# Attention and a gated FFN in one kernel: the last pair's value copies, weight sums, batch order and event spacing changed

## The chip, the core and the metric

The kernel runs on one core of a Trainium2 chip. The metric is the device time of one execution in microseconds; three runs of the kernel before gave a median of 419.42 us (418.75 to 419.45).

## The reference

The inputs are q, k and v of 8 batches, 12 heads, 448 tokens and head dimension 64 (float32), and three weight matrices. What is computed:

```python
scores = q @ k.T / sqrt(64)                  # per batch and head
attn   = maximum(scores, 0) ** 2 / 448
x      = (attn @ v)                          # heads side by side: 3584 tokens x 768
gate   = maximum(x @ w_gate, 0)              # 768 -> 1536
val    = x @ w_val                           # 768 -> 1536
out    = (gate * val) @ w_out                # 1536 -> 768
```

There is no softmax: a ReLU and a square stand in its place, so the scores need no row sums, and all scale factors are put into later copies.

## The kernel before

All matmuls are in bf16 with float32 sums in PSUM, which is used as eight banks of 512 words (`banks`). Four matmuls that each use a quarter of TensorE's array (64 x 64) are issued together by `mm4`; four such matmuls over 448 columns are called a pass here.

**Scores and values.** A score event (`scores_event`, lines 670 and 232 to 251) is one pass into a pair of banks, a ReLU by ScalarE into a buffer `r_sb` (line 234), and a squaring by VectorE into an `attn` buffer (line 235). Seven score events make one quarter-batch unit (`qd`), of which a batch has three. A values event (`values_event`) is seven passes over `attn` and v into another pair of banks, and then copies out of PSUM into `x`. Both kinds of event take their banks from one rotation, banks 0-1 and 2-3 in turn (`sc_later`). So the second event after a values event needs the banks that the values were summed in. There are two `attn` buffers and four `r_sb` buffers.

Batches before 6 copy the values with `values` (line 265): ScalarE takes one bank, VectorE the other. Batches 6 and 7 use `values_by_parity` (line 272): even heads lie in the lower 64 partitions and odd heads in the upper 64. ScalarE copies the lower half of both banks (line 277) and VectorE the upper half of both (line 278); two more VectorE copies (279 and 280) repeat each result in the other half.

**Interleaving.** The stage of a batch runs through the gate and value units of the batch before (`gv_unit`, 12 units of 12 passes). Each unit sums into a pair of banks from the rotation 6-7, 4-5, and ends with a ReLU by ScalarE (line 321) and a product by VectorE (line 322) into `hT`. The events of the attention are put between the unit's passes at places that a function chooses ahead of time: `evenly` (line 704) spreads them by their number over the unit's passes, whether an event is one pass or seven. `spread` then issues everything in that order. Each engine's queue is in the order in which the program is written (`pin`). From batch 5 on, the scores and values of batches 5, 6 and 7 form one stream (`stream`, line 730), which the two last stages share.

**Loads.** `later_loads(b)` (line 722) is put at a place in a stage: two small copies by POOL that wait for the transposes of k and q (`hold`, line 683), then the loads of v for the next batch and of q and k for the one after, all issued by POOL.

**The output in block form.** For batches 2 and 3, 4 and 5, and 6 and 7, `out_pair` computes the output product with Winograd's scheme: seven block products in place of eight, at the price of sums of blocks. The blocks of `hT` are A11, A12 (the rows of the second half of d_ff) for the first batch's columns, and A21, A22 for the second's; `sums` (line 420) makes S1 = A21 + A22, A21 = A11 - A21, A11 = S1 - A11 and A12 = A12 - A11, each in two halves of rows by VectorE (line 422). Every product (`product`) is 12 matmuls for a tile of 128 tokens. ScalarE copies finished banks to an `attn` buffer (line 414), VectorE adds the other bank (line 418), and the result is stored from there by POOL, SP or, at the end, ScalarE's queue (`store_rows`, line 432). The `attn` buffers are then given to attention again. In the last pair the tokens are taken in two groups, tiles 0 and 1, then 2 and 3.

**The last pair in block form too.** `gv_pair` (line 510) does the gate and value products of batches 6 and 7 by the same scheme, in three groups of two units; each group is fourteen products of 24 matmuls. x11 to x22 are the blocks of the two batches' tokens (`token_sums`), a11 to a22 those of the weights, and s1, s2, s4 the weight sums (`block_sums`). The sums for the first group are made by VectorE during the output product before (line 792); those for the second and third group by POOL, at the start of the first and second group (`begun`, line 579). ScalarE keeps intermediate banks (line 540), and VectorE adds (line 544) and multiplies (545, 566) into `hT`.

Of the kernel before, what the change touches and what calls it, by code (L numbers as in the profile page):

```python
# [16 lines left out]
def kernel(  # L17
# [254 lines left out]
    def values_by_parity(b, qd, ps):  # L272

        value_passes(b, qd, ps, 0, NC)
        even, odd = (x_of[b][e][qd] for e in range(2))
        lo, hi = (p for _, p in HALVES)
        pin(nc.scalar.activation(even[lo], ps[lo, :, :S], AF.Copy, scale=float(lam)))
        pin(nc.vector.tensor_scalar(odd[hi], ps[hi, :, :S], float(lam), None, ALU.mult))  # L278
        pin(nc.vector.tensor_copy(even[hi], even[lo]))
        pin(nc.vector.tensor_copy(odd[lo], odd[hi]))  # L280
# [92 lines left out]

    def out_pair(b0, S1, extra=()):

# [6 lines left out]

        hT = hT_of[b0]
        A11, A12, A21, A22 = (hT[:, r * KH:r * KH + KH, c * S:c * S + S] for c in range(2) for r in range(2))
        tiles = [(t * 128, WHOLE) for t in range(S // 128)] + [(S - HALF, HALF)]
# [33 lines left out]

        def sums(o, a, b, op, s):  # L420
            for f in (slice(0, KH // 2), slice(KH // 2, KH)):
                pin(nc.vector.tensor_tensor(o[:, f, s], a[:, f, s], b[:, f, s], op))  # L422

        def store_rows(t, r, c0, c1, engines):
# [8 lines left out]

        pool, sync = ((e, e) for e in (nc.gpsimd, nc.sync))
        both, ends = (nc.gpsimd, nc.sync), (nc.sync, nc.scalar)
        for group in (((0, 1), (2, 3)) if last else ((0, 1, 2, 3),)):
            early = last and group[-1] == 3
            cols = slice(tiles[group[0]][0], sum(tiles[group[-1]]))
            sums(S1, A21, A22, ALU.add, cols)
            sums(A21, A11, A21, ALU.subtract, cols)  # L440
            for t in group:
                product(P, t, A11, B11, True)
                keep(t, 0, 0)
            sums(A11, S1, A11, ALU.subtract, cols)
            for t in group:
                product(Q, t, A12, B21, True)
                add(t, 0, 0)
                if early:
                    store_rows(t, 0, 0, 1, pool)
            sums(A12, A12, A11, ALU.subtract, cols)  # L450
            for t in group:
                product(P, t, A11, T2, False)
                keep(t, 0, 1)
                more(1)
# [3 lines left out]
            for t in group:  # L458
                product(P, t, A21, B12, False)
# [22 lines left out]
    def head_sums(o, a, b, op, engine):  # L482
        pin(engine.tensor_tensor(o, a, b, op))

    def token_sums(b0):

        x11, x21, x12, x22 = (x_of[b0 + j][e] for j in range(2) for e in range(2))
        t1, t2, t4 = (quads(flat(t, HP, S)) for t in (kn_b[0], qn_b[0], v_b[1]))
        ops = [[lambda q=q: head_sums(t1[q], x12[q], x11[q], ALU.subtract, nc.vector) for q in range(NQ)],
               [lambda q=q: head_sums(t2[q], x22[q], t1[q], ALU.subtract, nc.vector) for q in range(NQ)],  # L490
               [lambda q=q: head_sums(x12[q], x22[q], x12[q], ALU.subtract, nc.vector) for q in range(NQ)],
               [lambda q=q: head_sums(t4[q], x21[q], t2[q], ALU.subtract, nc.vector) for q in range(NQ)]]
        return (x11, x21, x22, t1, t2, x12, t4), ops
# [6 lines left out]

    def block_sums(m, s, engine):

        a11, a12, a21, a22 = blocks(m)
        s1, s2, s4 = s
        return [lambda: head_sums(s1, a21, a22, ALU.add, engine),
                lambda: head_sums(s2, s1, a11, ALU.subtract, engine),
                lambda: head_sums(a21, a11, a21, ALU.subtract, engine),
                lambda: head_sums(s4, a12, s2, ALU.subtract, engine)]

    def gv_pair(b0, xs, sets):  # L510

# [14 lines left out]
        for g in range(KF // 4):  # L526
            for op in (sets.begun(g) if g < 2 else ()):
                op()
            ms = (2 * g, 2 * g + 1)
# [6 lines left out]
            def out(n, i, c):  # L536
                return hT[:, 2 * ms[n] + i, c * S:c * S + S]

# [17 lines left out]
            for n in range(2):  # L556
                product(n, PQ[n][1], s[n][0], t1, True)
            for n in range(2):
                product(n, PQ[n][0], a[n][2], t3, False)
                keep(n, 2)  # L560
                add(n, 2, 1, 1)
            for n in range(2):
                product(n, PQ[n][0], a[n][3], t4, False)
                g_sb = gpool.tile([128, S], BF16, name="g_sb")
                pin(nc.scalar.activation(g_sb, banks[:, PQ[n][0], :S], AF.Relu))
                pin(nc.vector.tensor_tensor(out(n, 1, 0), banks[:, PQ[n][0] + 1, :S], g_sb, ALU.mult))  # L566
            for n in range(2):
                product(n, PQ[n][1], s[n][2], x22, False)
                add(n, 1, 0, 1)

    class Sets:
# [158 lines left out]
    def stream(b0, b1):  # L730

        e = []
        for b in range(b0, b1):
            for n in range(NT):
                if n % NC == 2 and (b, n) != (b0, 2):
                    vb, qd = (b, n // NC - 1) if n > NC else (b - 1, NQ - 1)
                    e.append((b, n, values_event(vb, qd)))
                e.append((b, n, scores_event(b, n)))
# [46 lines left out]
    def thirds(t):  # L785
        return [t[:, 2 * n:2 * n + 2, :].rearrange("p a s -> p (a s)")[:, 0:HP * 128].rearrange("p (g f) -> p g f", f=128)
                for n in range(3)]
# [3 lines left out]
                  .rearrange("p (g f) -> p g f", f=128) for _ in range(3)]])  # L791
    w0, w1 = (block_sums(m, sets.of(m), nc.vector) for m in range(2))
# [32 lines left out]
```

## Time and profile before

| | |
|---|---|
| median of three runs | 419.42 us (418.75 to 419.45) |
| profiled execution, whole | 420.81 us |
| its span, first to last instruction | 418.8 us |
| mean granted TensorE clock in the span | 0.993 |
| DMA traffic | 44.20 MB, mean 106 GB/s |
| stage of batches 5 to 7 | about 224.6 to 313.2 us |
| output block of batches 4 and 5 | about 313.2 to 337.2 us |
| gate and value pair of batches 6 and 7 | about 337.2 to 387.0 us |
| output block of batches 6 and 7, and tail | about 387.0 to 418.8 us |

The profile is one execution. PE is TensorE's matmuls and PEld its weight loads, DVE is VectorE, ACT ScalarE, POOL GpSimd, SP SyncE; a q behind a name (SPq, ACTq) is the engine's queue, where DMAs are issued. A row of the timeline has the start, the time from the first start to the last end, the engine, the line in the code, the operation and its tiles, the count, and in brackets the idle time of the engine ahead of it and who ended it. Neighbouring matmuls overlap, so the time of a row is longer than the distance to the next. A row of the chain (start, duration, what) can be a DMA on its way. A row of grouped instructions has the count, then the busy time and the mean in ns of one, then the idle time before.

### The profile page before, as it was taken

Reading aid. Unit: us, or ns where it says so; the run is one execution under the profiler, and the core shown is the slowest. Engines: PE = TensorE matmul, PEld = TensorE weight load, DVE = VectorE, ACT = ScalarE, POOL = GpSimd, SP = SyncE. Lnnn points to the kernel's source line nnn. Section 1 sums busy time; section 2 is a strip of 40 time slices with the busy share of each in tenths; the row PEclk is TensorE's granted clock in tenths of the full one; section 3 lists DMA queues with packets and bytes.
Section 4 is the critical chain, followed back from the end, with each engine's and each line's share of the span. In section 5 each row is a group of like instructions: output and inputs, shape, how many; then the busy total and the mean of one; then the engine's idle time right before and its main releaser. Section 6 shows DMA issues by size and latency. Waiting matters only on the chain.

```text
span 418.8 us, 17139 instructions
## 1 busy us (share of the span) xinstructions
PE 399.2 (95%) x7728; PEld 297.3 (71%) x7728; DVE 293.0 (70%) x493; ACT 243.3 (58%) x351; POOL 111.9 (27%) x155
## 2 busy tenths in 40 slices
PE   8899999999999999999999899999999999999894
PEld 4467777899887777777776577666667766677573
DVE  4985777347675998677924668887769966695651
ACT  4962886256765776886335678888773243334231
POOL 8823501250051410230007100020000189910030
PEclk9999999999999999999999999999999999999998
DMA  9999999989899793592709920750000170000053
GB/s 157 180 201 196 201 207 201 145 133 183 87 123 223 112 165 56 86 172 26 132 4 240 193 35 21 114 70 2 4 2 2 48 221 3 2 3 3 2 171 95
DMA packets 85929, 44.20 MB, mean 106 GB/s; under 512 B 54464, under 2 KB 83744, under 8 KB 85856
## 3 DMA queue, kind: packets, MB, share of 16 engines
q0 software_dynamic: 48704, 29.96, 48.5%
q1 hardware_dynamic: 36560, 12.66, 16.8%
q8 instruction: 60, 0.98, 1.0%
q10 hardware_dynamic: 592, 0.49, 0.5%
q14 instruction: 13, 0.11, 0.1%
HBM read 47.19 MB, written 11.01 MB: 139 GB/s over the span
## 4 chain that ended last, share of the span: by engine, by line
PE 63%; DMA 20%; DVE 7%; issue 4%; ACT 2%; POOL 2%; DVEq 0%; SPq 0%; POOLq 0%; ACTq 0%
PE ps L72 63%; DMA gv<-in_moe_w_val_dram 9%; DMA vn<-in_v_dram 5%; DMA out_dram<-attn 2%; DMA out_dram<-o_ring 2%; DVE kqT L544 2%; DVE hT L545 1%; DMA kn<-in_k_dram 1%; DMA kqT<-kr 1%; POOL vn L116 1%; POOL qn L116 1%; ACT r_sb L234 1%; DVE hT L566 1%; DVE x L278 1%; ACT kqT L540 0%
## 5 line engine op out<-in xcount | busy, mean ns | idle before, releaser
L72 PE MATMUL ps<-x,gv 64*64 64x448 bf16 x3648 | 209.1, 351 | 1.2 <-ACT o_ring L354 0.5
L72 PEld LDWEIGHTS <-gv 64*64 64x64 bf16 x4032 | 153.5, 107 | 48.4 <-issue 5.7
L234 ACT ACTIVATE r_sb<-ps 128x896 bf16<-128x896 f32 x168 | 148.8, 928 | 27.4 <-PE ps L72 24.3
L235 DVE TENSOR_TENSOR attn<-r_sb 128x896 bf16<-128x896 bf16 x168 | 102.6, 623 | 41.8 <-ACT r_sb L234 34.1
L72 PEld LDWEIGHTS <-hT 128*64 128x64 bf16 (+1 forms) x1536 | 71.9, 109 | 23.3 <-issue 2.7
L72 PE MATMUL ps<-kqT 64*64 64x448 bf16 x672 | 74.0, 353 | 8.2 <-ACT r_sb L234 2.4
L72 PE MATMUL ps<-wo,hT 64*64 64x384 bf16 (+2 forms) x1248 | 75.5, 315 | 0.8 <-issue 0.5
L322 DVE TENSOR_TENSOR hT<-ps,g_sb 128x448 bf16<-128x448 f32 x72 | 44.5, 619 | 13.9 <-ACT g_sb L321 13.5
L321 ACT ACTIVATE g_sb<-ps 128x448 bf16<-128x448 f32 x72 | 39.2, 546 | 23.3 <-PE ps L72 23.1
L414 ACT ACTIVATE attn<-ps 128x384 f32<-128x384 f32 (+1 forms) x48 | 21.7, 451 | 49.6 <-PE ps L72 49.6
L432 POOL DMA_DIRECT2D out_dram<-attn x24 | 13.1, 548 | 134.5 <-ACT attn L414 128.7
L72 PEld LDWEIGHTS <-kqT 64*64 64x64 bf16 x672 | 32.4, 107 | 21.3 <-issue 12.9
L72 PEld LDWEIGHTS <-vn 64*64 64x64 bf16 (+1 forms) x840 | 33.5, 107 | 10.0 <-issue 1.1
L72 PE MATMUL ps<-attn,vn 64*64 64x448 bf16 x672 | 38.3, 349 | 0.0
L418 DVE TENSOR_TENSOR attn<-ps,attn 128x384 f32<-128x384 f32 (+1 forms) x36 | 16.9, 502 | 23.1 <-ACT attn L414 14.1
L540 ACT ACTIVATE kqT<-ps 128x896 f32<-128x896 f32 x18 | 16.5, 918 | 26.7 <-PE ps L72 26.7
L683 POOL COPY flag<-kqT 128x1 bf16<-128x1 bf16 x12 | 2.8, 242 | 102.9 <-DMA kqT<-kr 70.2
L544 DVE TENSOR_TENSOR kqT<-ps,kqT 128x896 f32<-128x896 f32 x18 | 19.5, 1082 | 14.8 <-ACT kqT L540 11.4
L116 POOL DMA_DIRECT2D vn<-in_v_dram x36 | 23.6, 672 | 18.8 <-DMA wo<-in_moe_w_out_dram 9.9
L72 PE MATMUL ps<-o_ring,hT 128*64 128x384 bf16 (+1 forms) x288 | 22.2, 306 | 1.5 <-DVE hT L422 1.4
L268 ACT ACTIVATE x<-ps 128x448 bf16<-128x448 f32 x15 | 8.2, 544 | 17.8 <-PE ps L72 17.8
L263 DVE COPY x<-x 64x896 bf16<-64x896 bf16 x36 | 14.6, 407 | 2.0
(99 smaller groups left out, 299.4 us busy)
## 6 DMA issues: line engine op xcount, KB each, us to landing
out_dram<-attn SPq DMA_DIRECT2D x16, 192.0 KB, 4.6
out_dram<-attn POOLq DMA_DIRECT2D x16, 192.0 KB, 4.5
kn<-in_k_dram POOLq DMA_DIRECT2D x7, 384.0 KB, 8.0
qn<-in_q_dram POOLq DMA_DIRECT2D x7, 384.0 KB, 10.6
vn<-in_v_dram POOLq DMA_DIRECT2D x14, 192.0 KB, 7.8
out_dram<-o_ring POOLq DMA_DIRECT2D x14, 192.0 KB, 5.5
wo<-in_moe_w_out_dram POOLq DMA_DIRECT2D x2, 1152.0 KB, 16.9
kn<-in_k_dram POOLq DMA_DIRECT2D x7, 288.0 KB, 9.3
```

The lines of the kernel that those rows point to most:

```text
L72: pin(nc.tensor.matmul(o, lhsT=l, rhs=r, start=start, stop=stop, skip_group_check=True))
L116: pin(nc.gpsimd.dma_start(out=o, in_=i))
L234: pin(nc.scalar.activation(r, src, AF.Relu))
L235: pin(nc.vector.tensor_tensor(dst, r, r, ALU.mult))
L263: pin(nc.vector.tensor_copy(x1[p], x0[other]))
L321: pin(nc.scalar.activation(g_sb, o[0], AF.Relu, scale=float(out_scale)))
L322: pin(nc.vector.tensor_tensor(hT[:, mf, col:col + S], o[1], g_sb, ALU.mult))
L414: pin(nc.scalar.activation(out_of(t, r, c), bank(P, t), AF.Copy))
L418: pin(nc.vector.tensor_tensor(o, bank(Q, t), o, ALU.add))
L432: pin(engines[c].dma_start(out=rows[:, c0:c1, :], in_=src))
L540: pin(nc.scalar.activation(held(n, j), both(PQ[n][0]), AF.Copy))
L544: pin(nc.vector.tensor_tensor(k, both(PQ[n][1]), k, ALU.add))
```

## The change

- `values_by_parity`: for each half of the partitions ScalarE copies the first bank and VectorE the second, four copies of 64 x 448 in place of two of 64 x 896.
- The places of the events in the last two stages come from a new function, `paced`. It counts passes, one for a score, seven for a values event, one for each pass of a unit, and gives each score the same number of passes; a values event lies half a period behind the score before it, and the next score half a period behind that.
- `later_loads(5)` is put at the fifth unit of its stage in place of the third.
- `token_sums` takes the two batches of the last pair in the other order, and `gv_pair` writes the results to `hT` with the column blocks exchanged, so that the first batch's place in the scheme is taken by batch 7.
- The weight sums of the second and third group are VectorE's, later in the group: behind the products of s1 with t1. No sum is left to POOL.
- In the third group VectorE makes S3 = A11 - A21 and, in two parts, S1 for the first two token tiles. `out_pair` of the last pair then leaves these out and keeps S2 and S3 in tiles of their own (the places of t2 and t1), where A11 and A21 were overwritten.
- The last stores are given to other queues: the second batch's first column half of the last two tiles to ScalarE's queue alone (SP and ScalarE before), the first batch's second half of tile 2 to SP alone (SP and ScalarE before).

```diff
-        pin(nc.scalar.activation(even[lo], ps[lo, :, :S], AF.Copy, scale=float(lam)))
-        pin(nc.vector.tensor_scalar(odd[hi], ps[hi, :, :S], float(lam), None, ALU.mult))
+        for x, p in ((even, lo), (odd, hi)):
+            pin(nc.scalar.activation(x[p, 0, :], ps[p, 0, :S], AF.Copy, scale=float(lam)))
+            pin(nc.vector.tensor_scalar(x[p, 1, :], ps[p, 1, :S], float(lam), None, ALU.mult))
...
+    def half_sums(o, a, b, op, s, halves=(0, 1)):
+        for f in (slice(n * KH // 2, (n + 1) * KH // 2) for n in halves):
+            pin(nc.vector.tensor_tensor(o[:, f, s], a[:, f, s], b[:, f, s], op))
...
-        A11, A12, A21, A22 = (hT[:, r * KH:r * KH + KH, c * S:c * S + S] for c in range(2) for r in range(2))
+        A11, A12, A21, A22 = quarters(b0)
+        S2, S3 = apart or (A11, A21)
...
-            sums(S1, A21, A22, ALU.add, cols)
-            sums(A21, A11, A21, ALU.subtract, cols)
+            if not last:
+                half_sums(S1, A21, A22, ALU.add, cols)
+                half_sums(S3, A11, A21, ALU.subtract, cols)
+            elif early:
+                half_sums(S1, A21, A22, ALU.add, cols)
             for t in group:
                 product(P, t, A11, B11, True)
                 keep(t, 0, 0)
-            sums(A11, S1, A11, ALU.subtract, cols)
+            half_sums(S2, S1, A11, ALU.subtract, cols)
...
-                        store_rows(t, 1, 0, 1, ends)
+                        store_rows(t, 1, 0, 1, act)
...
-                        store_rows(t, 0, 1, 2, ends)
+                        store_rows(t, 0, 1, 2, sync if tiles[t][1] == WHOLE else ends)
...
-        x11, x21, x12, x22 = (x_of[b0 + j][e] for j in range(2) for e in range(2))
+        x11, x21, x12, x22 = (x_of[b0 + 1 - j][e] for j in range(2) for e in range(2))
...
         for g in range(KF // 4):
-            for op in (sets.begun(g) if g < 2 else ()):
-                op()
...
-                return hT[:, 2 * ms[n] + i, c * S:c * S + S]
+                return hT[:, 2 * ms[n] + i, (1 - c) * S:(2 - c) * S]
...
             for n in range(2):
                 product(n, PQ[n][1], s[n][0], t1, True)
+            if ms[1] < KF // 2 - 1:
+                for op in sets.begun(g):
+                    op()
+            else:
+                A11, A12, A21, A22 = quarters(b0)
+                begun = slice(0, 2 * WHOLE)
+                half_sums(S1, A21, A22, ALU.add, begun, (0,))
+                half_sums(S3, A11, A21, ALU.subtract, slice(0, S))
...
+            if ms[1] == KF // 2 - 1:
+                half_sums(S1, A21, A22, ALU.add, begun, (1,))
...
-            return [op for m in (2 * g + 2, 2 * g + 3) for op in block_sums(m, self.of(m), nc.gpsimd)]
+            return [op for m in (2 * g + 2, 2 * g + 3) for op in block_sums(m, self.of(m))]
...
+    def paced(units, u1, events):
+
+        places, todo, t = [], list(events), 0
+        at = [(u, n) for u in range(u1) for n in range(len(units[u]))]
+        scores = sum(passes == 1 for *_, passes in events)
+        period = (len(at) + sum(passes for *_, passes in events)) / scores
+        due = period / 2
+        for u, n in at:
+            while todo and t >= due:
+                *_, e, passes = todo.pop(0)
+                places.append((u, min(n, len(units[u]) - 4), e))
+                t += passes
+                due += period / 2 if todo and (passes > 1) != (todo[0][3] > 1) else period
+            t += 1
+        return places + [(u1 - 1, len(units[u1 - 1]) - 4, e) for *_, e, _ in todo]
...
-            events = evenly(units, 0, last + b % 2, [e for _, _, e in todo])
+            events = paced(units, last + b % 2, todo)
...
-        events.append(({2: 10, 5: 2}.get(b, 3), 1, lambda b=b: later_loads(b)))
+        events.append(({2: 10, 5: 4}.get(b, 3), 1, lambda b=b: later_loads(b)))
...
-    gv_pair(B - 2, xs, sets)
-    out_pair(B - 2, S1)
+    S2, S3 = (flat(t, KH, S) for t in (qn_b[0], kn_b[0]))
+    gv_pair(B - 2, xs, sets, S1, S3)
+    out_pair(B - 2, S1, apart=(S2, S3))
```

More of the change, by code (lines that the diff above doesn't have):

```diff
@@ L372, in weight_sums, with quarters, out_pair @@
         pin(nc.vector.tensor_tensor(o, a, b, op))
-    def out_pair(b0, S1, extra=()):
+    def half_sums(o, a, b, op, s, halves=(0, 1)):
+        for f in (slice(n * KH // 2, (n + 1) * KH // 2) for n in halves):
+            pin(nc.vector.tensor_tensor(o[:, f, s], a[:, f, s], b[:, f, s], op))
+    def quarters(b0):
+        hT = hT_of[b0]
+        return [hT[:, r * KH:r * KH + KH, c * S:c * S + S] for c in range(2) for r in range(2)]
+    def out_pair(b0, S1, extra=(), apart=None):
         last, extra = b0 == B - 2, list(extra)
@@ L432, in store_rows @@
                 pin(engines[c].dma_start(out=rows[:, c0:c1, :], in_=src))
[L434 removed]
+        pool, sync, act = ((e, e) for e in (nc.gpsimd, nc.sync, nc.scalar))
         both, ends = (nc.gpsimd, nc.sync), (nc.sync, nc.scalar)
@@ L449, in out_pair @@
                     store_rows(t, 0, 0, 1, pool)
-            sums(A12, A12, A11, ALU.subtract, cols)
+            half_sums(A12, A12, S2, ALU.subtract, cols)
             for t in group:
-                product(P, t, A11, T2, False)
+                product(P, t, S2, T2, False)
                 keep(t, 0, 1)
@@ L458, in out_pair @@
             for t in group:
-                product(P, t, A21, B12, False)
+                product(P, t, S3, B12, False)
                 keep(t, 1, 1)
@@ L477, in out_pair, with head_sums @@
                     if early:
-                        store_rows(t, 0, 1, 2, ends)
+                        store_rows(t, 0, 1, 2, sync if tiles[t][1] == WHOLE else ends)
                     else:
                         store_rows(t, 0, 0, 2, both)
-    def head_sums(o, a, b, op, engine):
-        pin(engine.tensor_tensor(o, a, b, op))
+    def head_sums(o, a, b, op):
+        pin(nc.vector.tensor_tensor(o, a, b, op))
     def token_sums(b0):
-        x11, x21, x12, x22 = (x_of[b0 + j][e] for j in range(2) for e in range(2))
+        x11, x21, x12, x22 = (x_of[b0 + 1 - j][e] for j in range(2) for e in range(2))
         t1, t2, t4 = (quads(flat(t, HP, S)) for t in (kn_b[0], qn_b[0], v_b[1]))
[L489 to L492, printed above, removed]
+        ops = [[lambda q=q: head_sums(t1[q], x12[q], x11[q], ALU.subtract) for q in range(NQ)],
+               [lambda q=q: head_sums(t2[q], x22[q], t1[q], ALU.subtract) for q in range(NQ)],
+               [lambda q=q: head_sums(x12[q], x22[q], x12[q], ALU.subtract) for q in range(NQ)],
+               [lambda q=q: head_sums(t4[q], x21[q], t2[q], ALU.subtract) for q in range(NQ)]]
         return (x11, x21, x22, t1, t2, x12, t4), ops
```

22 lines of the change are left out of this document (9 added, 13 removed).

## The prediction

> **What bounds the kernel now.** I read the page's shares and clock line first, then the windows view (where TensorE stands or runs slowly), then the timeline around each such place.
>
> ```profile
> span 418.8 us, 17139 instructions
> PE 399.2 (95%) x7728; PEld 297.3 (71%) x7728; DVE 293.0 (70%) x493; ACT 243.3 (58%) x351; POOL 111.9 (27%) x155
> 238.00:240.00 2.00, 1.26 (x16) 0.84 (x19) 1.85 (x5) 0.77 (x1) 0.00 (x0) 0.74 1.52 194
> 240.00:242.00 2.00, 2.00 (x28) 1.36 (x24) 1.43 (x3) 0.84 (x3) 0.00 (x0) 0.50 1.47 188
> 242.00:244.00 2.00, 2.00 (x44) 1.50 (x40) 0.63 (x1) 1.61 (x3) 0.00 (x0) 0.91 0.54 69
> 390.00:396.00 6.00, 4.58 (x58) 2.92 (x56) 4.79 (x11) 0.98 (x2) 0.00 (x0) 1.00 0.00 0
> ```
>
> TensorE is busy 95% of the span, so only its stalls and slow stretches can be won. In a windows row the columns are PE, PEld, DVE, ACT, POOL, granted clock, DMA share and GB/s. From 238 to 244 us the clock falls to 0.74, 0.50 and 0.91: 0.26 x 2 + 0.50 x 2 + 0.09 x 2 = 1.70 us of work lost. From 390 to 396 us TensorE also stands still, for 1.42 us, and the clock stays at 1.00. What stands ahead of the slow stretch:
>
> ```profile
> 224.59 0.57 PE L72 MATMUL ps<-x,gv 64*64 64x448 bf16 x8
> 227.43 8.72 DMA out_dram<-attn
> 229.62 1.33 PE L72 MATMUL ps<-x,gv 64*64 64x448 bf16 x24
> 230.75 0.39 PE L72 MATMUL ps<-kqT 64*64 64x448 bf16 x4
> 236.46 1.16 DVE L235 TENSOR_TENSOR attn<-r_sb 128x896 bf16<-128x896 bf16 x2 [3.56 <-DMA out_dram<-attn]
> 238.07 0.61 DVE L269 CAST x<-ps 128x448 bf16<-128x448 f32 x1
> 238.74 0.41 PE L72 MATMUL ps<-kqT 64*64 64x448 bf16 x2 [2.09 <-DVE x L269]
> ```
>
> The last store of the first block-form output (issued 227.43, 8.72 us on its way) holds an attention buffer. VectorE wants that buffer for the eighth score of batch 5, waits 3.56 us for it, and with it waits everything queued behind: two squarings, one gate product, the copy of the first values (L269). TensorE needs that copy's PSUM bank and starts again at 238.74. I call four matmuls a pass: 24 matmuls from 229.62 to 230.75, so 0.189 us a pass.
>
> **Part 1, events spaced by passes, stage of batches 5 to 7 (224.6 to 313.2 us).** In the built program's TensorE order, the score that stalls (the eleventh) comes after 61 passes now and after 67 in the changed kernel; the eighth score after 37 passes now, 48 then. Nothing ahead of the release changes: POOL's and SP's lists up to there, and what each entry waits for, are the same in both builds. So "one part's loads later" moves nothing (POOL is held by its own queue, not by the place in the source), the store still lands at 236.15, and L269 still ends near 238.69: eighth and ninth squaring, a gate product and L269 are queued on VectorE there in the new order too. TensorE arrives at 224.6 + 67 x 0.189 = 237.26 instead of 224.6 + 61 x 0.189 = 236.1. It has then done 6 passes more when it restarts at 238.74: **-1.13 us**. Its wait is 1.48 us. Of today's 2.6 us (236.1 to 238.74) 2.09 show as idle, since matmuls already issued run out first; of the 1.48 some 1.0 to 1.2 will, less than the 1.42 after which the clock stayed at 1.00: the slow stretch goes, **-1.70 us**.
>
> **Part 2, the values' copies and what follows them.**
>
> ```profile
> 264.17 1.52 PE L72 MATMUL ps<-attn,vn 64*64 64x448 bf16 x28
> 265.50 0.95 PE L72 MATMUL ps<-x,gv 64*64 64x448 bf16 x16
> 265.74 0.91 ACT L277 ACTIVATE kn<-ps 64x896 bf16<-64x896 f32 x1 [0.88 <-PE ps L72]
> 266.69 1.09 DVE L278 TENSOR_SCALAR kn<-ps 64x896 bf16<-64x896 f32 x1 [1.01 <-ACT kn L277]
> 267.83 0.38 PE L72 MATMUL ps<-kqT 64*64 64x448 bf16 x4 [0.81 <-DVE kn L278]
> 247.74 0.55 ACT L268 ACTIVATE x<-ps 128x448 bf16<-128x448 f32 x1 [0.79 <-PE ps L72]
> 247.78 0.63 DVE L269 CAST x<-ps 128x448 bf16<-128x448 f32 x1 [0.17 <-PE ps L72]
> 313.17 7.03 PE L72 MATMUL ps<-wo,hT 128*64 128x384 bf16 x96
> L234 ACT ACTIVATE r_sb<-ps 128x896 bf16<-128x896 f32 x168 | 148.8, 928 | 27.4 <-PE ps L72 24.3 <-ACT g_sb L321 1.2 <-ACT r_sb L234 0.8
> ```
>
> Today both engines read both banks, and VectorE begins (266.69) only when ScalarE has ended: the bank is free 2.33 us after the last value pass (265.50 to 267.83). Bank by bank they run side by side, as L268 and L269 do at 247.74. ScalarE needs two of 0.55, VectorE two of about 0.62 with some 0.07 of overlap, from 0.24 after the passes: free at 0.24 + 1.17 + 0.03 = 1.44 us. That is 0.9 us less. But the new spacing puts a score directly behind the value passes and the next, which needs their bank, one or two passes later; today ten to thirteen passes lie between. So the wait is not 2.33 - 1.32 = 1.01 any more, but 1.44 - 0.38 = 1.06 with one pass between (three times), 1.44 - 0.57 = 0.87 with two (once), 1.44 - 0.19 = 1.25 with none (batch 6, first): 5.30 together. Batch 5's second and third values keep the old copies (free at 0.24 + 0.63 + 0.03 = 0.90) and waited for nothing; now 0.90 - 0.38 = 0.52 and 0.90 - 0.57 = 0.33. For VectorE being late (regrouping copies and gate products in its queue) I add 0.60, an estimate of one L322 or so. New: 6.75 us of waits. Now: from 238.74 to the output block at 313.17 are 74.43 us for 414 - 61 = 353 passes x 0.189 = 66.7, so 7.7 lost, less the clock's 1.70: 6.0. Difference **+0.75 us**: faster copies, nearly all spent on closer neighbours. ScalarE and VectorE keep up between values: a score every 6.2 to 6.4 passes is 1.2 us, a ReLU 0.93.
>
> Stage: -1.13 - 1.70 + 0.75 = -2.08. Bounds: -3.0 (VectorE never late, shorter copies) and -0.4 (slow stretch stays).
>
> **Part 3, weight sums from POOL to VectorE (337 to 387 us).**
>
> ```profile
> 337.23 0.57 PE L72 MATMUL ps<-kn,gv 64*64 64x448 bf16 x8
> 353.80 0.95 PE L72 MATMUL ps<-kn,gv 64*64 64x448 bf16 x8
> 370.91 0.57 PE L72 MATMUL ps<-kn,gv 64*64 64x448 bf16 x8
> 387.01 1.17 PE L72 MATMUL ps<-wo,hT 128*64 128x384 bf16 x12
> 348.71 1.09 DVE L544 TENSOR_TENSOR kqT<-ps,kqT 128x896 f32<-128x896 f32 x1 [4.00 <-ACT kqT L540]
> 349.83 1.77 DVE L545 SCALAR_TENSOR_TENSOR hT<-kqT 128x448 bf16<-128x448 f32 x1
> 383.45 0.63 DVE L545 SCALAR_TENSOR_TENSOR hT<-kqT 128x448 bf16<-128x448 f32 x1
> 358.36 0.57 PE L72 MATMUL ps<-kn,gv 64*64 64x448 bf16 x8 [0.58 <-DVE kqT L544]
> 326.31 0.55 DVE L483 TENSOR_TENSOR x<-gv 128x768 bf16<-128x768 bf16 x1
> 328.43 1.15 DVE L483 TENSOR_TENSOR kr<-qr,kr 128x896 bf16<-128x896 bf16 x2
> ```
>
> The first three rows and 387.01 bound three equal groups: 16.57, 17.11 and 16.10 us. POOL works in the first two only, and there VectorE's L545 takes up to 1.77 us against 0.63 without POOL. VectorE falls behind and TensorE waits (358.36). Without POOL the first two should take 16.10 each: -0.47 - 1.01 = **-1.5 us**. VectorE gets eight sums a group: four took 328.43 - 326.31 = 2.12, so 4.24 us. They stand in its queue where it was idle for 4.00 us, after an L545 that gets 0.3 shorter: they fit, with some 0.6 us to spare before TensorE meets the next L544. If they didn't fit, up to 2.8 us (1.4 a group) would come back.
>
> **Part 4, start of the last output block, and tail.**
>
> ```profile
> 382.32 1.09 DVE L544 TENSOR_TENSOR kqT<-ps,kqT 128x896 f32<-128x896 f32 x1 [4.28 <-ACT kqT L540]
> L422 DVE TENSOR_TENSOR kn<-hT 128x1344 bf16<-128x1344 bf16 x2 | 1.6, 849 | 0.0
> 388.38 1.08 DVE L544 TENSOR_TENSOR kqT<-ps,kqT 128x896 f32<-128x896 f32 x1
> 390.03 1.02 DVE L422 TENSOR_TENSOR vn<-hT 128x768 bf16<-128x768 bf16 x2
> 392.51 1.65 PE L72 MATMUL ps<-o_ring,hT 128*64 128x384 bf16 x18 [1.42 <-DVE hT L422]
> 410.46 5.68 SPq L432 DMA_DIRECT2D out_dram<-attn  x8
> 411.62 2.96 ACTq L432 DMA_DIRECT2D out_dram<-attn  x4
> out_dram<-attn SPq DMA_DIRECT2D x16, 192.0 KB, 4.6
> ```
>
> Today six half sums follow the last hT row (390.1), and TensorE waits 1.42 us for the fifth. In the new order four of them lie earlier. S3 and half of S1 stand in VectorE's idle time before the third group's adds (4.28 us; 2 x 0.85 + 0.55 = 2.25 of sums). S3 overwrites t1 and so waits until TensorE has passed the group's eighth product, at 370.91 + 8 x 16.10/14 = 380.1 and a run-out of 0.2; it ends at 382.0, before 382.32, and behind it in the queue is the add that TensorE's last products need: 0.3 us to spare, and what S3 is late beyond that would come on top. The other half of S1 stands before the last adds, which end 0.5 later, at 390.6. Then two sums, until 391.6. But A12 now holds the rows made last: the first Q product (from 388.96, 12 matmuls in 1.17 less the run-out, 0.081 each) stops at its fifth row until 390.65, ends 391.0, its neighbour at 392.0, and the block that began at 392.51 begins there: **-0.5 us** (bounds -1.0 and +0.3). In the tail SP issues eight stores in 5.68 us, 0.71 each, and is last; one goes to ScalarE's queue. Alone that is -0.7, and nothing if the two queues take turns; I take **-0.4 us**. The Trainium skill, Perfetto Trace Analysis, section "DMA Instruction — HWDGE (DVE, Sync)", says that the descriptor generator is locked for one issuer at a time; by that the tail would give 0 and the sum 0.4 us less. No row here decides it.
>
> **Sum.** -2.08 - 1.5 - 0.5 - 0.4 = -4.5 us. The profiled execution is 418.8 us of span in 420.81 us; the median of the runs is 419.42, and the same difference is taken off it: **414.9 us**. A measurement of this kernel can tell about 0.2%, 0.84 us.
>
> **Rivals.**
> *A: the slow stretch stays.* The stores land at another moment than here, or 1.1 us of standing already halves the clock. For: nothing between 1.42 (held) and 2.09 us (halved) was seen, and the landing is a DMA's. Against: 1.42 held. 414.9 + 1.7 = 416.6 us, chance 0.13.
> *B: the loads do come later* and the store lands in the 4.6 us median of its kind (the row above): about 1 us more is won, 413.9 us. Against: the same POOL list. Chance 0.04.
> *C: VectorE becomes the bound in the pair*: 1.5 not won and 2.8 given back: 414.9 + 4.3 = 419.2, no change. For: VectorE would be busy almost all of two groups. Against: the idle slots of 4.0 us. Chance 0.04.
> *D: slower; the two halves of the copies still run one after the other* (a bank or a semaphore orders them as now). Then the bank is free at 2.33, and the five waits are 2.14 + 1.76 + 3 x 1.95 = 9.75 instead of 5.30: 419.35. TensorE stands for 1.75 us at three of them and 1.94 at one, beyond the 1.42 that was harmless; each halving costs 1.7, and with one the kernel is slower, with four 426.2. It decides from a copy of about 2 us on. Against: 247.74 shows the pair side by side. Chance 0.06. The Trainium skill, TensorE: Matmul & The Clock Gate, section "What's actually happening", has the clock fall only after about 3.4 us of idle window; by that D would stay at 419.35 and A would not exist. The 2.09 us of standing ahead of 0.50 contradict it, so D and A keep their prices.
>
> **How the numbers follow.** Forecast 0.73, A 0.13, B 0.04, C 0.04, D 0.06. The range 412.9 to 417.2 takes in the forecast with its bounds, A and B, and leaves C, D out. Faster by over 0.2%: forecast, A, B and a part of C, 0.91; within: 0.03; slower: 0.06.
>
> **What would show it.** Part 1: idle near 237 us of 1.0 to 1.3, clock 1.00 from 238 to 244. Part 2: ACT and DVE copies of 64x448 at the same time, and seven TensorE waits of 0.3 to 1.1 us (less the run-out) behind value passes. Part 3: no L545 over 0.65 us, groups of about 16.1 us, no TensorE wait for L544. Part 4: a wait of about 0.9 us inside the first Q product, none for S2; the last SP store issued some 0.5 us sooner against the last matmul. Wrong would be: a granted clock under 1 behind a value copy (D), L544 late in the pair (C), the store landing before 235 (B).

## The result, and the profile after

The changed kernel takes 414.63 us in the median (414.24 to 415.19), the kernel before beside it 419.43 us: ratio 0.989, 95% interval 0.9873 to 0.9908. The forecast was 414.9. The profiled execution took 414.38 us.

The page of the changed kernel, first its span and the shares of the engines, then the windows view around 238 us (columns as in the prediction):

```profile
span 412.6 us, 17150 instructions
PE 397.6 (96%) x7728; PEld 293.4 (71%) x7728; DVE 298.8 (72%) x513; ACT 245.3 (59%) x357; POOL 82.5 (20%) x139
236.00:238.00 2.00, 1.41 (x26) 0.69 (x22) 1.90 (x5) 1.35 (x2) 0.00 (x0) 1.00 1.55 192
238.00:240.00 2.00, 2.00 (x52) 1.50 (x44) 1.66 (x4) 1.46 (x2) 0.00 (x0) 1.00 1.48 196
240.00:242.00 2.00, 2.00 (x48) 1.51 (x44) 1.51 (x3) 1.76 (x4) 0.00 (x0) 1.00 1.23 153
```

TensorE still misses 0.59 us ahead of 238, but the clock stays at 1.00 where it was 0.74 and 0.50. Rows of the timeline and, for the store, of the chain, in order of time; the comparison by stage rests on their starts:

```profile
223.83 0.95 PE L72 MATMUL ps<-x,gv 64*64 64x448 bf16 x16
226.50 8.56 DMA out_dram<-attn
236.95 0.38 PE L72 MATMUL ps<-kqT 64*64 64x448 bf16 x2 [0.25 <-ACT x L268]
237.66 0.38 PE L72 MATMUL ps<-kqT 64*64 64x448 bf16 x2 [0.34 <-DVE x L269]
282.16 1.10 ACT L278 ACTIVATE x<-ps 64x448 bf16<-64x448 f32 x2 [0.61 <-PE ps L72]
282.34 1.27 DVE L279 TENSOR_SCALAR x<-ps 64x448 bf16<-64x448 f32 x2
283.31 0.73 PE L72 MATMUL ps<-kqT 64*64 64x448 bf16 x4 [0.64 <-ACT x L278]
310.16 2.14 PE L72 MATMUL ps<-wo,hT 128*64 128x384 bf16 x24
334.22 2.46 PE L72 MATMUL ps<-kr,gv 64*64 64x448 bf16 x48
350.25 2.47 PE L72 MATMUL ps<-kr,gv 64*64 64x448 bf16 x48
366.21 2.47 PE L72 MATMUL ps<-kr,gv 64*64 64x448 bf16 x48
382.31 2.79 PE L72 MATMUL ps<-wo,hT 128*64 128x384 bf16 x32
386.07 1.49 PE L72 MATMUL ps<-wo,hT 128*64 128x384 bf16 x16 [0.97 <-DVE hT L551]
387.39 2.12 PE L72 MATMUL ps<-o_ring,qn 128*64 128x384 bf16 x24
406.22 1.67 PE L72 MATMUL ps<-wo,hT 128*64 128x384 bf16 x24
405.32 4.60 SPq L437 DMA_DIRECT2D out_dram<-attn  x7
406.47 3.15 ACTq L437 DMA_DIRECT2D out_dram<-attn  x5
L551 DVE SCALAR_TENSOR_TENSOR hT<-kqT 128x448 bf16<-128x448 f32 x18 | 11.3, 625 | 0.6
345.70 1.09 DVE L550 TENSOR_TENSOR kqT<-ps,kqT 128x896 f32<-128x896 f32 x1 [0.35 <-ACT kqT L546]
```

| | before, us | after, us | difference | forecast |
|---|---|---|---|---|
| stage of batches 5 to 7 | 88.58 | 86.33 | -2.25 | -2.08 |
| output block of batches 4 and 5 | 24.06 | 24.06 | 0 | 0 |
| gate and value pair | 49.78 | 48.09 | -1.69 | -1.5 |
| start of the last output block to the first S2 product | 5.50 | 5.08 | -0.42 | -0.5 |
| start of the last product to the end of the span | 7.44 | 6.38 | -1.06 | -0.4 |

Together -5.42. The spans differ by 6.2; of the remaining 0.8, 0.76 is that the stage starts at 223.83 in place of 224.59. The change touches nothing ahead of it, and in the profiled executions below this start lies between 223.11 and 224.69 us, without regard to what was changed.

### The profile page after: what moved, and what is told of

It reads as the page before. It is cut to its first block, busy times and chain, and to the rows that moved or that the text cites. A ratio compares the mean times of both kernels' runs of the same rounds, so it can differ in the third digit from the quotient of the medians.

```text
span 412.6 us, 17150 instructions
## 1 busy us (share of the span) xinstructions
PE 397.6 (96%) x7728; PEld 293.4 (71%) x7728; DVE 298.8 (72%) x513; ACT 245.3 (59%) x357; POOL 82.5 (20%) x139
## 4 chain that ended last, share of the span: by engine, by line
PE 63%; DMA 18%; issue 11%; DVE 3%; POOL 2%; ACT 1%; DVEq 0%; POOLq 0%; ACTq 0%
PE ps L72 63%; DMA gv<-in_moe_w_gate_dram 7%; DMA wo<-in_moe_w_out_dram 4%; DMA vn<-in_v_dram 3%; DMA out_dram<-attn 3%; DMA kn<-in_k_dram 1%; DVE kqT L550 1%; POOL vn L116 1%; DVE hT L551 0%; POOL qn L116 0%; POOL out_dram L437 0%; POOL gv L116 0%; DVE hT L580 0%; ACT x L278 0%; ACT qr L278 0%
## 5 line engine op out<-in xcount | busy, mean ns | idle before, releaser
L72 PE MATMUL ps<-x,gv 64*64 64x448 bf16 x3552 | 201.6, 349 | 0.8 <-ACT r_sb L234 0.3
L234 ACT ACTIVATE r_sb<-ps 128x896 bf16<-128x896 f32 x168 | 150.2, 925 | 25.6 <-PE ps L72 22.4
L72 PE MATMUL ps<-kqT 64*64 64x448 bf16 x672 | 79.0, 351 | 6.2 <-ACT r_sb L234 2.2
L72 PEld LDWEIGHTS <-hT 128*64 128x64 bf16 (+1 forms) x1440 | 65.4, 109 | 21.4 <-issue 2.7
L72 PE MATMUL ps<-wo,hT 64*64 64x384 bf16 (+2 forms) x1200 | 71.5, 316 | 1.7 <-DVE hT L551 1.0
L72 PEld LDWEIGHTS <-kqT 64*64 64x64 bf16 x672 | 34.0, 106 | 21.0 <-issue 12.8
L72 PE MATMUL ps<-o_ring,hT 128*64 128x384 bf16 (+1 forms) x240 | 18.5, 306 | 0.1
```

The source lines that it names most:

```text
L72: pin(nc.tensor.matmul(o, lhsT=l, rhs=r, start=start, stop=stop, skip_group_check=True))
L234: pin(nc.scalar.activation(r, src, AF.Relu))
```

## The experiments

Two sets ran, each on one chip beside the kernel before: 418.82 us in the first set (418.71 in the second). The changed kernel's 414.63 was measured earlier, beside 419.43, so a difference from it is told with the trace's where that matters.

**The old copies.** `values_by_parity` as in the kernel before, everything else as changed:

```diff
-        for x, p in ((even, lo), (odd, hi)):
-            pin(nc.scalar.activation(x[p, 0, :], ps[p, 0, :S], AF.Copy, scale=float(lam)))
-            pin(nc.vector.tensor_scalar(x[p, 1, :], ps[p, 1, :S], float(lam), None, ALU.mult))
+        pin(nc.scalar.activation(even[lo], ps[lo, :, :S], AF.Copy, scale=float(lam)))
+        pin(nc.vector.tensor_scalar(odd[hi], ps[hi, :, :S], float(lam), None, ALU.mult))
```

> The changed kernel with the old value copies (ScalarE the lower half of both banks, then VectorE the upper half of both), the new spacing kept. Theory (the copies' length against the distance of the next-but-one score sets the wait): the bank comes free 2.33 us after the value passes instead of 1.53, so the five waits of batches 6 and 7 are 2.14 + 1.76 + 3 x 1.95 = 9.75 us instead of the 5.75 measured: about 4.0 us slower than the changed kernel, 418.6 us, with TensorE idle 1.75 us at three places. Rival 1 (a stand of between 1.42 and 2.09 us already halves the clock): up to 1.7 us more for each halved window, 420.3 to 425, and a granted clock of 0.5 behind value passes. Rival 2 (the waits are slack that ScalarE's and VectorE's load would take anyway): under 1 us slower, below 415.7.

Measured: 419.59 us (418.19 to 421.73), ratio to the kernel before 1.0013 (0.9988 to 1.0038). Without the new copies nothing of the gain is left. Rows of its timeline behind the value passes of batches 6 and 7, and of its windows:

```profile
266.07 0.38 PE L72 MATMUL ps<-kqT 64*64 64x448 bf16 x4 [1.94 <-DVE kn L278]
288.12 0.38 PE L72 MATMUL ps<-kqT 64*64 64x448 bf16 x4 [1.76 <-DVE x L278]
263.45:266.86 3.41, 1.47 (x33) 0.83 (x29) 2.46 (x5) 2.07 (x3) 0.00 (x0) 1.00 0.59 135
266.86:270.28 3.42, 3.42 (x44) 2.23 (x40) 1.78 (x3) 1.99 (x3) 2.95 (x5) 0.50 0.39 47
283.93:287.34 3.41, 2.43 (x52) 1.69 (x45) 1.88 (x4) 2.62 (x4) 0.00 (x0) 1.00 0.00 0
```

The five waits (1.94, 1.57 and 1.76 three times) are the ones that rival D foresaw, each 0.2 us shorter, and 1.1 us above those of the changed kernel (0.64 at 283.31). Only the first wait is followed by a halved stretch. The third, of 1.76 us, is not: half of it lies in each of two windows (the last section). Six of the ten executions have a mean clock of 0.994, the other four 0.998 or 0.999. Those four average 418.80 us, near the 418.6 of the theory; the six average 420.38, so rival 1 came beside it, in some of the executions.

**The old spacing.** `evenly` in place of `paced`, everything else as changed:

```diff
-            events = paced(units, last + b % 2, todo)
+            events = evenly(units, 0, last + b % 2, [e for *_, e, _ in todo])
```

> The changed kernel with the old even spacing of events, everything else new. Theory (the new spacing wins 1.3 us plus the clock's 1.7 at the store wait and then gives back some 5 us in waits behind value passes, which the new copies alone would nearly have removed): the stall of 2.1 us at the store wait and its slow stretch come back, +2.9; the waits behind value passes fall from 6.6 us to about 1.5; together about 2 us faster than the changed kernel, 412.6 us. Rival (the spacing itself is what makes the change faster): 2.8 us or more slower, 417.4 or more.

Measured: 412.51 us (411.06 to 413.62), ratio 0.9847 (0.981 to 0.9883). That is 2.1 us less than the changed kernel, and 6.3 less than the kernel before beside it, where the changed kernel gained 4.8: the new spacing costs more than it brings. In the traces the stage takes 85.59 us in place of 86.33, with a halved stretch of the clock in it. TensorE's waits in the stage, its end, and two windows:

```profile
237.82 0.58 PE L72 MATMUL ps<-kqT 64*64 64x448 bf16 x2 [2.14 <-DVE x L269]
276.67 0.38 PE L72 MATMUL ps<-kqT 64*64 64x448 bf16 x4 [0.43 <-ACT r_sb L234]
297.28 0.38 PE L72 MATMUL ps<-kqT 64*64 64x448 bf16 x4 [0.24 <-ACT r_sb L234]
309.21 1.98 PE L72 MATMUL ps<-wo,hT 128*64 128x384 bf16 x22
234.37:237.78 3.41, 1.31 (x26) 0.70 (x19) 2.23 (x4) 1.29 (x2) 0.00 (x0) 1.00 1.52 196
237.78:241.20 3.42, 3.38 (x40) 2.14 (x43) 2.65 (x5) 1.55 (x3) 0.00 (x0) 0.50 1.48 189
```

The wait for the store is back, 2.14 us, and in this execution the halved clock with it. But no wait for a value copy is left. From 237.82 to 309.21 are 71.39 us; 353 passes of 0.189 take 66.7 and the clock 1.70, so 3.0 us are lost, where the kernel before lost 6.0 with the same spacing and the old copies, and the changed kernel 6.9.

**The loads really later, in the kernel before.** Putting `later_loads(5)` two units later changed nothing: with its argument set back to 2 the changed kernel builds into the same instructions with the same waits on every engine. To make the loads later, POOL must wait for something. A small copy of an element that the seventh squaring writes does it, put behind that squaring by the later place:

```diff
+        if b == B - 3:
+            late = const.tile([128, 1], BF16, name="late")
+            pin(nc.gpsimd.tensor_copy(late, attn_of(b, 0)[:, 2 * NC - 1, 0:1]))
...
-        events.append(({2: 10, 5: 2}.get(b, 3), 1, lambda b=b: later_loads(b)))
+        events.append(({2: 10, 5: 4}.get(b, 3), 1, lambda b=b: later_loads(b)))
```

> The kernel before, with the loads of stage 5 truly later: POOL first copies one element of the attention buffer that the seventh score writes, so the loads of v and of q and k start about 233 us instead of 226.4. Theory (the loads stretch the last store to 8.7 us): the last store lands near 232 instead of 236.2, the eighth squaring does not wait, neither the stall of 2.1 us nor the slow stretch is there: 4.2 us faster than the kernel before, 415.2 us. Rival (the store is slow of itself, by the sixteen stores ahead of it): it lands near 236 as before and the time stays at 419.4; the loads then may be late for the transposes, at most some us slower.

Measured: 416.01 us (415.52 to 416.73), ratio 0.9934 (0.9907 to 0.996). POOL, VectorE and the clock in its timeline and windows, and the last store's line in the DMA view (KB, us from issue to landing), first of the kernel before, then of this run:

```profile
233.02 0.19 POOL L727 COPY late<-attn 128x1 bf16<-128x1 bf16 x1 [6.47 <-DVE attn L235]
233.14 0.62 DVE L235 TENSOR_TENSOR attn<-r_sb 128x896 bf16<-128x896 bf16 x1 [0.18 <-ACT r_sb L234]
236.00:240.00 4.00, 4.00 (x91) 2.95 (x86) 3.59 (x6) 3.81 (x6) 3.21 (x5) 1.00 1.39 164
out_dram<-attn SPq DMA_DIRECT2D x1, 96.0 KB, 8.7
out_dram<-attn SPq DMA_DIRECT2D x1, 96.0 KB, 5.2
```

The loads now start at 233.55. The store lands after 5.2 us instead of 8.7, VectorE squares without waiting for it (0.18 us, and for ScalarE), TensorE has no gap near 238, and the clock stays up. So the loads are what stretched the store. The halved clock is gone with the wait; one execution without it does not show that the wait caused it, but the windows of the last section bear that out. The gain is 2.8 us and not the 4.2 expected, which counted a halved stretch for every execution of the kernel before.

**Both: even spacing and loads held back, in the changed kernel.** The diff of the spacing and the copy for POOL together; the changed kernel has the later place already.

> The changed kernel with even spacing and with the loads truly later as in the run above. Theory: both gains add, since even spacing costs only the store wait: 412.6 less 4.2 = 408.4 us. Rival (ScalarE and VectorE become the bound once TensorE does not wait, being 37 to 40 us busy in 40 us of the stage): 410.5 or more, with TensorE waiting for the ReLUs (L234) instead.

Measured: 410.08 us (409.21 to 411.18), ratio 0.9792 (0.9763 to 0.9821); its profiled execution has waits of 0.43 and 0.24 us in the stage, both for the ReLU (L234) as the rival has it, and no other, and the stage takes 81.44 us (224.48 to 305.92). That is 1.7 us more than the 408.4 expected, less than the rival's 410.5. Of the 1.7, 1.4 is that the expectation took 4.2 us for the held loads where the run above showed 2.8.

**The weight sums back on POOL**, at the start of groups 0 and 1 (the two helpers, which get the engine as an argument again, are left out here):

```diff
         for g in range(KF // 4):
+            for op in (sets.begun(g) if g < 2 else ()):
+                op()
...
-            if ms[1] < KF // 2 - 1:
-                for op in sets.begun(g):
-                    op()
-            else:
+            if ms[1] == KF // 2 - 1:
...
-            return [op for m in (2 * g + 2, 2 * g + 3) for op in block_sums(m, self.of(m))]
+            return [op for m in (2 * g + 2, 2 * g + 3) for op in block_sums(m, self.of(m), nc.gpsimd)]
```

> The changed kernel with one part undone: the weight sums of the next group are done by GpSimd at the start of groups 0 and 1, as in the kernel before, and not by VectorE. Everything else stays as changed. Theory (the adds and the weight sums beside them share something when GpSimd does the sums, and VectorE's room is large enough to take them): the gv pair goes from 48.1 us back to about 49.3 to 49.8, the fused adds (scalar_tensor_tensor hT<-kqT) from a mean of 625 ns back to about 850, waits for them reappear in groups 0 and 1, and the time is 1.2 to 1.7 us above the changed kernel's 414.63: 415.8 to 416.3. Rival (the pair got faster through the swapped batches alone): no difference, 414.6.

Measured: 416.7 us (415.8 to 417.73), ratio 0.9952 (0.9924 to 0.9979). That is 0.4 above the highest time that was expected. Rows of the timeline, and the group of L553, the fused product (`scalar_tensor_tensor`, a ReLU and a product in one instruction; the expectation calls it the fused add):

```profile
333.40 2.46 PE L72 MATMUL ps<-kr,gv 64*64 64x448 bf16 x48
348.84 0.57 PE L72 MATMUL ps<-kn,x 64*64 64x448 bf16 x8 [0.35 <-DVE kqT L552]
354.52 1.33 PE L72 MATMUL ps<-qr,gv 64*64 64x448 bf16 x24 [0.58 <-DVE kqT L552]
383.18 2.14 PE L72 MATMUL ps<-wo,hT 128*64 128x384 bf16 x24
L553 DVE SCALAR_TENSOR_TENSOR hT<-kqT 128x448 bf16<-128x448 f32 x18 | 15.4, 854 | 0.6
```

The pair takes 49.78 us again, as before, with the batches still swapped, and the same instruction takes 854 ns in the mean in place of 625. Of the nine that run while POOL sums, eight take 0.94 to 1.78 us; the others take 0.62 to 0.65. The Trainium skill, GPSIMD Engine Reference, section "1. Specifications", says that GpSimd shares its SBUF interfaces with VectorE and that they contend when VectorE's instruction has two SBUF inputs. This agrees: the fused product has two inputs in SBUF, and those beside POOL's sums are the long ones. That it is these interfaces that they share was not measured by itself.

**The early sums put back** to the start of the last output block, the batches still swapped:

```diff
-            if not last:
-                half_sums(S1, A21, A22, ALU.add, cols)
-                half_sums(S3, A11, A21, ALU.subtract, cols)
-            elif early:
-                half_sums(S1, A21, A22, ALU.add, cols)
+            half_sums(S1, A21, A22, ALU.add, cols)
+            half_sums(S3, A11, A21, ALU.subtract, cols)
...
-            else:
-                A11, A12, A21, A22 = quarters(b0)
-                begun = slice(0, 2 * WHOLE)
-                half_sums(S1, A21, A22, ALU.add, begun, (0,))
-                half_sums(S3, A11, A21, ALU.subtract, slice(0, S))
...
-            if ms[1] == KF // 2 - 1:
-                half_sums(S1, A21, A22, ALU.add, begun, (1,))
```

> The changed kernel with the sums S1 and S3 of the last output block put back where the block starts; the batches stay swapped in the block form and S2 and S3 stay in tiles of their own. Theory (by the traces, the early sums bring the first S2 product 0.42 us nearer to the start of the block): 5.5 us again from the block's start to the first S2 product, time 0.4 us above the changed kernel: 415.0. A rival (the sums at the start of the block delay the adds, and the tail too): up to 1.5 us above, 416.1. A second rival (the wait for hT is what decides, whoever did the sums): 414.6.

Measured: 414.92 us (414.74 to 415.58), ratio 0.9917 (0.9884 to 0.995). The start of its last block:

```profile
382.50 2.79 PE L72 MATMUL ps<-wo,hT 128*64 128x384 bf16 x32
385.66 1.49 PE L72 MATMUL ps<-wo,hT 128*64 128x384 bf16 x16 [0.38 <-DVE hT L548]
388.00 1.17 PE L72 MATMUL ps<-o_ring,qn 128*64 128x384 bf16 x12 [0.85 <-DVE qn L377]
```

5.50 us to the S2 product, as in the kernel before, where the changed kernel takes 5.08: 0.42 us, 0.3 in the median, is all that these sums bring. They turn the two waits of 0.38 (hT's last rows) and 0.85 us (S2) into the one of 0.97.

**The last stores on their old queues:**

```diff
-                        store_rows(t, 1, 0, 1, act)
+                        store_rows(t, 1, 0, 1, ends)
...
-                        store_rows(t, 0, 1, 2, sync if tiles[t][1] == WHOLE else ends)
+                        store_rows(t, 0, 1, 2, ends)
```

> The changed kernel with the last output block's stores on their old queues: the last rows alternate between SyncE and ScalarE, as in the kernel before. Theory as predicted: the tail behind the last product 0.4 us longer, 415.0. By the two traces (7.44 us before, 6.38 after): 1.06 us longer, 415.7. Rival (both queues share one descriptor generator, so which engine issues makes no difference): 414.6.

Measured: 415.78 us (415.55 to 417.82), ratio 0.9939 (0.9912 to 0.9966). The tail in its timeline:

```profile
406.49 1.66 PE L72 MATMUL ps<-wo,hT 128*64 128x384 bf16 x24
405.59 5.66 SPq L437 DMA_DIRECT2D out_dram<-attn  x8
406.75 2.94 ACTq L437 DMA_DIRECT2D out_dram<-attn  x4
```

From the last product to the end of the span (413.9) it is 7.4 us again. So the allotment is worth the whole 1.06, and not the 0.4 forecast. Three of the twelve stores change queues by it; what is left on SP's queue, which ends last, is seven in place of eight.

**The best version: the even spacing, the loads held back, and the halves of S1 and S2 in another order.** The second half of S1 moves out of the pair; behind the last adds come S2's first half, S1's second, S2's second:

```diff
-            half_sums(S2, S1, A11, ALU.subtract, cols)
+            if last and not early:
+                half_sums(S2, S1, A11, ALU.subtract, cols, (0,))
+                half_sums(S1, A21, A22, ALU.add, cols, (1,))
+                half_sums(S2, S1, A11, ALU.subtract, cols, (1,))
+            else:
+                half_sums(S2, S1, A11, ALU.subtract, cols)
...
-            if ms[1] == KF // 2 - 1:
-                half_sums(S1, A21, A22, ALU.add, begun, (1,))
```

> The changed kernel with the events spaced evenly again and with the other part's loads held back until the store ahead of them has landed (410.08 us), and in addition the first half of S2 and the second half of S1 ordered so that the adds of the last group come first and S2's halves follow at once. Theory (the 0.97 us for which TensorE is idle ahead of the first A12 product of the last block is the wait for VectorE's S2): the idle time falls to about 0.45 and the time to 409.6. Rival (that wait is set by the last adds alone): 410.1.

Measured: 408.78 us (408.4 to 408.95), ratio 0.9769 (0.9731 to 0.9806), against 0.989 for the changed kernel. The start of its last block:

```profile
376.92 2.79 PE L72 MATMUL ps<-wo,hT 128*64 128x384 bf16 x32
380.08 1.49 PE L72 MATMUL ps<-wo,hT 128*64 128x384 bf16 x16 [0.37 <-DVE hT L556]
381.41 2.12 PE L72 MATMUL ps<-o_ring,qn 128*64 128x384 bf16 x24
```

4.49 us instead of 5.08, in the changed kernel and in the fourth experiment alike: the 0.97 was the last adds standing behind a half of S1 in VectorE's queue, not a wait for S2 as the expectation had it. The sums still end in time for S2's product. The median is 1.3 us below that of the fourth experiment, which ran on another chip; this order explains 0.6 of it. The stages are equally long (81.44 and 81.45). In the two profiled executions the rest lies ahead of the stage, which starts 1.16 us earlier here without any edit there.

## Why the prediction was right, point by point

The mechanisms were the ones forecast, and each part that was given a size has been undone alone; the swapped batches and the tiles apart were not. Of the sizes, several were off and partly cancelled: that the total came within 0.3 us of the measured median is partly luck.

- **Part 1, the pacing at the store: -1.13 forecast, -1.45 measured.** The changed kernel comes from 223.83 to 237.66 with 67 passes: 13.83 - 12.66 = 1.17 us lost, where 1.48 were foreseen (before: 14.15 - 11.53 = 2.62). The store was issued 2.67 us into the stage and took 8.56 us, where it was 2.84 and 8.72 before; it landed 0.33 us sooner. That is not the edit's doing; without it, the forecast -1.13 is met. Only 0.59 us show as idle, not 1.0 to 1.3: TensorE restarts in two steps, as ScalarE and VectorE free one bank each.
- **Part 1, the halved clock: -1.70 forecast, right for the two profiled executions and too much for the medians.** This term was mis-sized. In the 28 executions of the kernel before that ran beside the experiments the mean granted clock was 0.992 to 0.995 in 12 (means 419.90 and 420.35 us by set) and 0.996 to 0.999 in 16 (418.34 and 417.95). A halved stretch of 3.41 us lowers the mean over the span by 0.004. So the stretch is there in about 12 of 28, and its removal is worth some 0.73 in the mean. The count is rough, since the mean also holds a fall behind the last product (0.50 from 416.45 on in the trace of before), and the old spacing's profiled execution has the stretch at a mean of 0.996. The page had shown a hint: the profiled execution was 1.4 us above the median. Rival A did not come; its bound of 1.1 us was not tested by the 0.59 us left. The prediction priced the clock by how long TensorE stands at one place; the last section shows that this is not what decides.
- **Part 2: +0.75 forecast, +0.90 measured.** ScalarE and VectorE do copy side by side (282.16 and 282.34): ScalarE's two end at 283.26, VectorE's at 283.61, and TensorE restarts at 283.31 in the first bank. Behind value passes five waits show: 0.83, 0.45 and three times 0.64 us. Each is 0.42 below its forecast (1.25, 0.87 and 1.06), so these were foreseen rightly, with 0.42 us in which TensorE still runs out. Batch 5's two waits (0.52 and 0.33) do not show. The stage beyond its passes and the store's wait is 86.33 - 414 x 0.189 - 1.17 = 6.91 us, 6.75 foreseen. Not all of the 6.91 need be such waits: the fourth experiment's stage, with waits of only 0.43 and 0.24, takes 81.44 - 414 x 0.189 = 3.2 us beyond its passes. So the close agreement of this sum is in part luck. That the copies' gain is "nearly all spent on closer neighbours" is shown by the second experiment: it is spent on the spacing. The copies alone take 6.0 to 3.0, the spacing then adds 3.9.
- **Part 3: -1.5 forecast, -1.69 measured.** The three groups take 16.03, 15.96 and 16.10 us. The eight sums fit: the add behind them at 345.70 waits 0.35 us for ScalarE, not for them. Rival C did not come.
- **Part 4, start of the block: -0.5 forecast, -0.42 measured**, with the one wait at the place foreseen, 0.97 us.
- **Part 4, tail: -0.4 forecast, -1.06 measured**, outside the bounds of -0.7 and 0. This was the most mis-sized term. The eight stores of before took SP 5.68 us, 0.71 each; the seven take 4.60, 0.66 each. So one store less is 0.71, as in the working, and the others came 0.05 closer; nothing of it was given back, although ScalarE's queue issued five beside them. My discount for queues that take turns had no row. The rule that the prediction takes from the Trainium skill (Perfetto Trace Analysis, section "DMA Instruction — HWDGE (DVE, Sync)") and by which the tail would have given 0 is not what these stores show.
- **The loads:** "one part's loads later" moved nothing, as the identical programs show. Rival B's price, about 1 us, was too small for loads that do come later: 2.8 us in the kernel before.
- **Rival D** did not come, but the old copies put its waits to the test: 419.35 was its price without a halved clock, and the four executions at 0.998 or 0.999 average 418.80. Its four halvings did not show: the three waits of 1.76 us, each cut by a window's edge in this trace, did not halve the clock.

With the measured sizes and 0.73 for the clock the sum is -1.45 - 0.73 + 0.90 - 1.69 - 0.42 - 1.06 = -4.45; the medians differ by 4.80. The 0.35 between them is not explained; it is less than the 0.84 us that a measurement can tell.

## What to carry to other kernels

When a copy that frees a bank gets faster, look next at how far away the next user of that bank is: here an edit of the same change moved it closer, and 3.9 us of a possible gain went into that. An edit that moves a DMA issue in the source is worth nothing if its queue was waiting for something else; compare the engine's list and its waits, and give the queue something to wait for where the transfer must be later. A stall that halves the clock in some executions should be priced by how often it does so, and a profiled execution that lies above the median of its runs is a sign that it may hold more than the usual run.

## What the runs showed of the hardware that was not expected

In the three traces with a stall that halved it, the clock is halved for 3.41 us at a time, and what decides is how much TensorE worked in the 3.41 us ahead. Four windows of the kernel before, then two of the old spacing, cut at the places where the clock changes and at whole numbers of such windows from there:

```profile
235.55:238.96 3.41, 1.32 (x28) 0.70 (x24) 2.39 (x5) 1.08 (x2) 0.00 (x0) 1.00 1.52 196
238.96:242.37 3.41, 3.41 (x44) 2.27 (x40) 2.43 (x5) 1.97 (x3) 0.00 (x0) 0.50 1.45 188
389.13:392.54 3.41, 2.00 (x28) 1.16 (x22) 3.38 (x8) 0.49 (x1) 0.00 (x0) 1.00 0.00 0
416.45:418.80 2.35, 0.00 (x0) 0.00 (x0) 0.00 (x0) 0.00 (x0) 0.00 (x0) 0.50 0.14 35
405.04:408.45 3.41, 1.89 (x35) 1.55 (x30) 0.85 (x2) 0.78 (x2) 0.00 (x0) 1.00 0.66 165
408.45:411.66 3.21, 0.00 (x0) 0.00 (x0) 0.00 (x0) 0.00 (x0) 0.00 (x0) 1.00 0.39 101
```

With 1.32 us of work here, 1.31 with the old spacing and 1.47 with the old copies, the next window is at 0.50, as it is from 416.45 on behind a window without any work; with 2.00 at 389.13, with 1.89 at 405.04 with the old spacing, and with 1.95 at 236.14 and 2.43 at 283.93 with the old copies, it stays at 1.00. 389.13 lies 44 windows behind 238.96, and so the wait of 1.42 us there falls into one window whole. A wait of 1.76 us cut in two by a window's edge did no harm, one of 1.94 us within a window did. That a single stand of about 2 us is enough by itself is ruled out by the end of the old spacing's trace: TensorE has stood since 406.9 and the clock is at 1.00 up to the end of the span at 411.66, 4.7 us later. The Trainium skill, TensorE: Matmul & The Clock Gate, section "What's actually happening", gives a free-running window of 3413 ns, which agrees; its condition of at least one idle window for the fall does not, since these windows held 1.3 to 1.5 us of work. That the windows' edges lie elsewhere in each execution, so that the same wait halves the clock in some and not in others, fits the 12 of 28; the edges of the executions without a trace were not seen. Where between 1.47 and 1.89 us of work the threshold lies is open.
